# Attention followed by two mixtures of experts on one core: values in three buffers, keys and queries loaded three units ahead, weight loads shifted by unit

## The chip, the cores and the metric

The kernel runs on one core of one Trainium2 chip. The metric is the device time of one execution in microseconds (us). Three executions of the kernel before took 487.59, 489.71 and 493.68 us, a median of 489.71 us.

## The reference

The inputs are q, k and v of shape (4, 8, 576, 64) in float32, so 4 batches and 8 heads of 576 positions.

1. **Attention.** Each head has two softmax attentions that are added. One works on queries, keys and values averaged over groups of 4 positions (144 of them), its output repeated four times. The other is local: a query sees the keys less than 4 positions away. The result is read as x, 2304 tokens by 512.
2. **Soft mixture (called MoE1 here).** logits = x @ phi with 32 slots; a softmax over tokens forms 4 slot inputs for each of 8 experts; each expert computes relu(s @ w1) @ w2 with w1 512x1024 and w2 1024x512; a softmax over slots mixes the slot outputs back into tokens.
3. **Top-2 mixture (MoE2).** A noisy router picks two of 8 experts for each token; each expert computes relu(x @ w1) @ w2 for its tokens, weighted and added into the output, 2304 by 512.

All 16 weight matrices of MoE1 (2 MB each in float32) are read, and 16 more for MoE2.

## The kernel before

**Units and periods.** Attention works on 16 units, each one batch and a pair of heads. Loop variable `p` (L592) runs from -1 to 14; a turn of it is called a period here. Each period goes through the order written out by hand in `SEQ` (L19). Every name there is a step with an offset (table `BL`, L554): step `f` with offset `o` works in period `p` on unit `p - o`. So one period holds parts of four units. After the loop, `TSEQ` (L21) is the hand-written order of the tail, which finishes units 13 to 15 and goes over into MoE1.

**Steps that matter here.**
- `ld` (`load`, L186): four DMAs that bring keys and queries of a unit, two heads each, in rows of 256 bytes, into tile `ld`, which has two buffers. Offset -2: in period p it loads unit p+2. It is the second name of `SEQ`. `load(0)` is issued ahead of the loop.
- `A0`, `A1` (`a_pe`, L230; offset -1): TensorE transposes the keys (A0) and the queries (A1) of unit p+1 out of `ld`.
- `lV` (`load_v`, L202; offset -1): four DMAs (five or six for a few units) bring the values of unit p+1 into one of two buffers `Vs`, unit u into `Vs[u % 2]`. It stands near the end of `SEQ`, behind `DP`.
- `VD` (`v_pe`, L266; offset 1) and `DP` (`d_pe`, L407; offset 1) are the steps that read the values: the averaged values, and the local attention's product.
- `W` (`flush`, L580): issues as many entries of the list `todo` as `NW[p]` says, here 1 in every period from p = 0. An entry is half of a matrix of MoE1, 1 MB. Eight matrices (16 halves) are on the list (`NPRE = 8`); 15 are issued in the loop and the last by the `W` of `TSEQ`.
- `SU_`, `ST`, `SS`, `SK`, `SE`: work on one whole batch for the slot softmax, so in one period of four each, from p = 5.

**Small loads.** Eight small DMAs (two router weights, six pieces of the noise) are issued one for each period from p = 5 (L595), at the start of the period. `phi` is loaded at the start of p = 0.

**Queues.** All these loads are issued by SyncE's queue (SP) in program order. A DMA whose buffer is not free yet makes SP wait, and everything behind it in the order too.

**After attention.** Step `R2` of `TSEQ` gives the memory of attention's buffers to `ring2` (L629): three more matrices of MoE1 (tiles w8a to w10b) are loaded there, each as soon as the tiles that lay there have been read. The last five matrices go through `ringa` and `ringb` (tile `wr`), buffers that come free as MoE1 uses the first matrices. `hidden` (L793) and `second` (L818) are the two layers of MoE1 on TensorE, expert after expert. Behind MoE1 come the router and MoE2 (`tile2`, L1047).

Of the kernel before, what the change touches and what calls it, by code (L numbers as in the profile page):

```python
# [7 lines left out]
F32 = mybir.dt.float32  # L8
# [7 lines left out]

CAP = 640

SEQ = """DM ld S DD A0 M a00 a01 A1 a110 XA a100 SD EL a101 ST a111 SK CP SS EX W VD EP01 MD V0 EP00 EP10 SU_ LG CD EP11  # L19
EP V1 LA ED0 DX SU KD ED1 DP lV x1 x0 DQ1 X0 SE DQ0 RD P0 X1 P1""".split()  # L20
TSEQ = """S:15 DD:13 XA:13 DM:14 CP:14 W EP01:14 EP00:14 SD:15 M:15 EL:15 EP10:14 EX:15 EP11:14 CD:14 ED0:14 MD:15 SU:15 VD:14 DP:14 V0:14 V1:14 EP:13  # L21
ED1:14 P0:15 P1:15 DD:14 DX:15 LG:13 X0:13 RD:15 x0:14 DM:15 x1:14 CP:15 LA:13 EP00:15 X1:13 EP01:15 EP11:15
CD:15 EP10:15 XA:14 ED0:15 VD:15 DP:15 V0:15 V1:15 ED1:15 DD:15 EP:14 x0:15 x1:15 LG:14 X0:14 XA:15 LG:15 EP:15 X0:15 LA:14
# [2 lines left out]
ON_V = ['k1', 'd1', 'a101', 'a111', 'v0']  # L26
ON_V_END = ['P0', 'k1', 'v0', 'v1']

NW = [1] * 15

SPIN = [2, 0, 1, 14, 6, 1]
NPRE = 8
# [6 lines left out]
def attn_moe_moe_kernel(ctx: ExitStack, tc: tile.TileContext, q, k, v, moe_phi, moe_w1, moe_w2,  # L39
                        w_gate, w_noise, noise, w1, w2, out, dbg=None):  # L40
    nc = tc.nc
    B, H, S, D = q.shape
    NT = B * S
    DM = H * D
# [11 lines left out]
    NU = len(units)  # L56
# [61 lines left out]
    with ExitStack() as tctx:  # L118
# [6 lines left out]
        a1 = actx.enter_context(tc.tile_pool(name="a1", bufs=1))  # L125
        wka = actx.enter_context(tc.tile_pool(name="wka", bufs=2))
        a2 = actx.enter_context(tc.tile_pool(name="a2", bufs=1))
        wk = actx.enter_context(tc.tile_pool(name="wk", bufs=2))
# [24 lines left out]
        P = a2.tile([128, NG, 64], F32, name="P")  # L153
        PdT = a2.tile([128, 2, 2, 144], F32, name="PdT")
        Vd = a2.tile([128, 2, 128], F32, name="Vd")
        Vs = [(a1, a2)[i].tile([128, 5, 2, D], F32, name=f"V{i}") for i in range(2)]
        four = a2.tile([128, 9, 32], F32, name="four")
        for a in range(2):
            as_ = slice(64 * a, 64 * a + 64)
# [24 lines left out]
        LD, KD, DQ, SD, SS, SB, PD, PL, XL, XT, XK = ({} for _ in range(11))  # L184

        def load(u):  # L186
            b, hp = units[u]
            t = ldp.tile([96, 2, 6, 2, D], F32, name="ld")
            for i, src in enumerate((k, q)):
                for h in range(2):  # L190
                    nc.sync.dma_start(out=t[:, i, :, h], in_=src[b, 2 * hp + h].rearrange("(c p) d -> p c d", c=6))
            LD[u] = t
# [8 lines left out]

        def load_v(u):  # L202
            b, hp = units[u]
            V = Vs[u % 2]
            hv = v[b, 2 * hp:2 * hp + 2]
            for h in range(2):
                for g2 in range(2):

                    j0, j1 = int(u == h == g2 == 0), 5 - int(u == NU - 1 and h == g2 == 1)
                    rows = slice(64 * g2, 64 * g2 + 64)  # L210
                    t0 = 58 * (2 * j0 + g2) - 3
                    nc.sync.dma_start(out=V[rows, j0:j1, h], in_=bass.AP(
                        tensor=hv.tensor, offset=hv.offset + (h * S + t0) * D,
                        ap=[[D, 64], [116 * D, j1 - j0], [1, D]]))
                    if j0:
                        nc.sync.dma_start(out=V[3:64, 0, h], in_=hv[h, 0:61])
                    if j1 < 5:
                        nc.sync.dma_start(out=V[64:121, 4, h], in_=hv[h, S - 57:S])

# [45 lines left out]

        def v_pe(u):  # L266

            V = Vs[u % 2]
            XL[u] = [ps.tile([128, 512], F32, name=n) for n in ("xa", "xb")]
            t = XL[u][0][:, 290:418]  # L270
            for d in range(2):
                for c in range(4):
                    nc.tensor.matmul(t[32 * c:32 * c + 32], four[:, 5 * d + c],
                                     V[:, c + d].rearrange("p h d -> p (h d)"), start=(d == 0), stop=(d == 1),
                                     skip_group_check=True)
            nc.tensor.matmul(XL[u][1][0:32, 290:418], four[:, 4], V[:, 4].rearrange("p h d -> p (h d)"), start=True,
                             stop=True, skip_group_check=True)
# [128 lines left out]

        def d_pe(u):  # L407
            b, hp = units[u]
            V = Vs[u % 2]
            xl = XL[u]  # L410
            PTv = PT.rearrange("p j g (a i h) -> p j g h a i", a=2, h=2)
            for j in range(5):
                for g in range(2):
                    gs = slice(64 * g, 64 * g + 64)
                    for h in range(2):
                        nc.tensor.matmul(xl[g][64 * h:64 * h + 64, 58 * j:58 * j + 58], V[gs, j, h],
                                         PTv[gs, j, g, h, :, 0:HQ], start=True, stop=True, skip_group_check=True)
# [131 lines left out]
        def ok(u):  # L549
            return 0 <= u < NU  # L550

        load(0)

        BL = {"ld": (load, -2, ()), "lV": (load_v, -1, ()), "EP": (e_pe, 2, ()), "LG": (logit_pe, 2, ()),  # L554
              "X0": (e_evac, 2, (0,)), "X1": (e_evac, 2, (1,)), "LA": (logit_add, 2, ()),
              "S": (b_s, 0, ()), "SD": (b_d, 0, ()), "M": (soft_m, 0, ()), "EL": (soft_s, 0, ()), "EX": (soft_e, 0, ()),
              "SU": (soft_l2, 0, ()), "P0": (soft_p, 0, (0,)), "P1": (soft_p, 0, (1,)), "MD": (soft_d1, 0, ()),
# [8 lines left out]
        for j in range(2):  # L566
            BL[f"a0{j}"] = (a_evac, -1, (0, 0, j))
            for h in range(2):
                BL[f"a1{h}{j}"] = (a_evac, -1, (1, h, j))
        for i in range(2):  # L570
            BL[f"x{i}"] = (d_evac, 1, (i,))
        MW, todo = {}, []
# [7 lines left out]
        def flush(n=99):  # L580
            for _ in range(min(n, len(todo))):
                todo.pop(0)()

        for i in range(NPRE):
            mload(ORDW[i], ringa if i < 3 else ringb)
        small = [(wgn[:, :, E * i:E * i + E], w.rearrange("(k p) e -> p k e", p=128))
                 for i, w in enumerate((w_gate, w_noise))]
# [4 lines left out]
        for p in range(-1, NU - 1):  # L592
            if p == 0:
                nc.sync.dma_start(out=phi, in_=moe_phi.rearrange("(k p) s -> p k s", p=128))
            if p >= 5 and small:  # L595
                o, i = small.pop(0)
                nc.sync.dma_start(out=o, in_=i)
            if p == 1:
                nc.gpsimd.memset(zero, 0.0)
            b4, r4 = divmod(p - 5, 4)  # L600
            for nm in SEQ:
                f, off, a = BL.get(nm, (None, 99, ()))
                if off is None:
                    if 0 <= b4 < B and r4 == a:
                        f(b4)
                elif ok(p - off):
                    f(p - off, *a)
                if nm == "W" and p >= 0:
                    flush(NW[p])
                if p == -1 and nm == "lV":  # L610
                    nc.gpsimd.memset(PT, 0.0)
                    nc.gpsimd.memset(Vd[:, 1], 0.0)
                    nc.gpsimd.memset(PdT[:, 1], 0.0)
                if p == -1 and nm == "DQ1":
                    nc.vector.memset(P, 0.0)
            if p == 0:
                hot(NHOT[0])
                nc.vector.tensor_scalar(trib, jp, 0.0, None, op0=ALU.is_gt)
                consts()
# [58 lines left out]
        for nm in TSEQ:  # L678
# [4 lines left out]
            else:  # L683
                n, u = nm.split(":")
                f, off, a = BL[n]
                f(int(u), *(a if off is not None else ()))
# [569 lines left out]
    for e in range(E):  # L1256
# [36 lines left out]
        elif nx is not None:  # L1293
# [4 lines left out]
            for n in range(NTILE):  # L1298
                i = s0 + n // 9
# [25 lines left out]
        for sl, n0, n1 in SCAT:  # L1325
            if sl // 5 == e:
                f = fill[sl % 5]
# [82 lines left out]
```

## Time and profile before

| | |
|---|---|
| median of three executions | 489.71 us |
| profiled execution: time, span | 488.25 us, 486.5 us |
| TensorE matmul, busy in the span | 458.1 us (94%) |
| VectorE, ScalarE, GpSimd, busy | 275.1, 270.5, 221.9 us |
| bytes moved by SP's queue | 90.50 MB |
| mean granted TensorE clock | 0.993 |

Busy times include pipelining and are no proof that an engine is the limit: the share is an average over stages with different limits. The stages by the trace: attention up to 159.94 us (first matmul of MoE1), MoE1 up to 192.42 us, router and first dispatch up to 207.94 us, then MoE2. In the rows further down, SPq is SyncE's queue issuing a DMA, PE is TensorE's matmuls and PEld its weight loads; a bracket at the end of a row gives how long the engine had been idle before and what released it.

### The profile page before, as it was taken

What the parts mean: (1) busy time and instruction counts of PE and PEld (TensorE: products, weight loads), DVE (VectorE), ACT (ScalarE), POOL (GpSimd) and SP (SyncE); (2) the same over time, 40 slices, a digit from 0 to 9 for tenths busy, and PEclk for the clock granted to TensorE, in tenths of its full rate; (3) what the DMA queues carried; (4) which work ended last, traced back from release to release, by engine and by line L of the source; (5) the groups of instructions that cost most, each with busy time, mean ns of one, the idle gap of its engine ahead of it and who ended that gap; (6) DMA issues with size and microseconds to landing.
All of it is one profiled execution on the core that took longest, in us unless ns stands there. A gap on an engine that the chain in (4) does not pass through costs nothing.

```text
span 486.5 us, 12430 instructions
## 1 busy us (share of the span) xinstructions
PE 458.1 (94%) x4765; PEld 355.7 (73%) x4765; DVE 275.1 (57%) x703; ACT 270.5 (56%) x699; POOL 221.9 (46%) x321
## 2 busy tenths in 40 slices
PE   6999998899888999999999999999999999999992
PEld 5788877778765543577777887887887877878882
DVE  6888676887875321886487463382552634615300
ACT  2687777777765112674484453672755646727310
POOL 7897667577631201084766677222222222212232
PEclk9999899999999999999999999999999999999998
DMA  8999999899979999999986843799958855333333
GB/s 161 234 245 204 249 207 204 222 224 232 251 212 377 378 394 395 372 341 353 355 236 183 244 67 62 214 357 265 274 98 220 201 129 139 45 43 45 44 44 46
DMA packets 107977, 104.19 MB, mean 214 GB/s; under 512 B 67722, under 2 KB 77642, under 8 KB 107914
## 3 DMA queue, kind: packets, MB, share of 16 engines
q1 hardware_dynamic: 101002, 90.50, 62.5%
q0 software_dynamic: 6912, 12.85, 17.6%
q8 instruction: 40, 0.66, 0.6%
q14 instruction: 23, 0.19, 0.1%
HBM read 83.60 MB, written 19.73 MB: 212 GB/s over the span
## 4 chain that ended last, share of the span: by engine, by line
PE 42%; issue 8%; POOL 2%; POOLq 2%; DVE 1%; DMA 1%; ACT 1%; DVEq 0%
PE y L1061 34%; PE gx L878 2%; PE h L1041 2%; POOL out_dram L1080 2%; POOLq L1086 1%; PE gx L1041 1%; DMA out_dram<-ys,idx 1%; PE xs L944 1%; DVE hl L1043 1%; PE xs L1022 0%; PE xs L941 0%; ACT ys L1072 0%; DVE wlo L1033 0%; PE gx L958 0%; ACT hh L1042 0%
## 5 line engine op out<-in xcount | busy, mean ns | idle before, releaser
L1061 PE MATMUL y<-whi,hl 128*128 128x512 f32 x320 | 127.3, 398 | 0.0
L1061 PE MATMUL y<-whi,hh 128*128 128x512 f32 x320 | 126.6, 396 | 0.4 <-ACT hh L1042 0.4
L1061 PE MATMUL y<-wlo,hh 128*128 128x512 f32 x320 | 126.6, 396 | 0.0
L1080 POOL DMA_INDIRECT out_dram<-ys,idx x40 | 64.6, 1614 | 108.5 <-ACT ys L1072 62.6
L1072 ACT ACTIVATE ys<-y,gt 128x512 f32<-128x512 f32 x40 | 27.4, 686 | 83.7 <-issue 46.9
L1033 DVE TENSOR_TENSOR wlo<-wr,whi 128x512 fp32r<-128x512 f32 x64 | 42.0, 692 | 49.3 <-ACT whi L1030 41.7
L1061 PEld LDWEIGHTS y<-wlo,hh 128*128 128x128 f32 x320 | 60.1, 188 | 12.9 <-issue 1.0
L1061 PEld LDWEIGHTS y<-whi,hl 128*128 128x128 f32 x320 | 60.1, 188 | 12.3 <-issue 2.1
L1061 PEld LDWEIGHTS y<-whi,hh 128*128 128x128 f32 x320 | 60.2, 188 | 11.8 <-ACT hh L1042 0.6
L1007 POOL DMA_INDIRECT tab<-stk,pos x36 | 35.8, 994 | 11.5 <-issue 10.4
L1043 DVE SCALAR_TENSOR_TENSOR hl<-h,hh 128x256 fp32r<-128x256 f32 (+1 forms) x64 | 31.4, 490 | 16.0 <-ACT hh L1042 10.6
L1043 DVE SCALAR_TENSOR_TENSOR hl<-gx,hh 128x256 fp32r<-128x256 f32 (+1 forms) x64 | 31.2, 488 | 10.7 <-ACT hh L1042 7.4
L1030 ACT ACTIVATE whi<-wr 128x512 fp32r<-128x512 f32 x64 | 36.9, 625 | 0.2
L1042 ACT ACTIVATE hh<-gx 128x256 fp32r<-128x256 f32 (+1 forms) x64 | 28.1, 439 | 15.0 <-PE gx L1041 12.0
L1042 ACT ACTIVATE hh<-h 128x256 fp32r<-128x256 f32 (+1 forms) x64 | 28.0, 437 | 12.5 <-PE h L1041 9.5
L236 PE MATMUL t<-idf,ld 96*128 96x96 f32 x192 | 23.7, 270 | 11.8 <-DMA ld<-in_q_dram 5.6
L1079 POOL MEMSET spacer<- 1x1 f32 x40 | 13.5, 338 | 40.9 <-issue 40.9
L236 PEld LDWEIGHTS t<-idf,ld 96*128 96x128 f32 x192 | 18.8, 153 | 16.4 <-DVE fa L166 4.3
L254 POOL TENSOR_TENSOR s<-Q 64x288 f32<-64x288 f32 x31 | 29.3, 945 | 2.4
L336 POOL TENSOR_TENSOR P<-El,su 64x350 f32<-64x350 f32 x31 | 24.4, 787 | 11.4 <-DVE Vd L226 4.9
L224 ACT ACTIVATE PT<-t 64x384 f32<-64x384 f32 (+1 forms) x64 | 25.9, 429 | 6.2 <-PE t L378 5.0
L926 DVE TENSOR_TENSOR oh<-iot,R 128x256 fp32r<-128x256 f32 (+2 forms) x50 | 20.5, 446 | 12.7 <-PE xs L944 10.3
(312 smaller groups left out, 877.9 us busy)
## 6 DMA issues: line engine op xcount, KB each, us to landing
wr<-in_moe_w_dram SPq DMA_DIRECT2D x88, 256.0 KB
wr<-in_moe_w_dram SPq DMA_DIRECT2D x40, 512.0 KB
wr<-in_moe_w_dram SPq DMA_DIRECT2D x16, 1024.0 KB
out_dram<-zero SPq DMA_DIRECT2D x20, 256.0 KB
V<-in_v_dram SPq DMA_DIRECT2D x62, 80.0 KB
ld<-in_k_dram SPq DMA_DIRECT2D x32, 144.0 KB
ld<-in_q_dram SPq DMA_DIRECT2D x32, 144.0 KB
XT<-tab SPq DMA_DIRECT2D x5, 320.0 KB
```

Of the source, the lines that this page charges most:

```text
L224: nc.scalar.activation(dst, src, AF.Copy)
L236: nc.tensor.transpose(t[:, 96 * c:96 * c + 96], ld[:, i, 3 * j + c].rearrange("p h d -> p (h d)"), idf[0:96, 0:96])
L254: nc.gpsimd.tensor_tensor(q2, q4[:, :, 0:2], q4[:, :, 2:4], op=ALU.add)
L336: eng.tensor_tensor(P[as_, :, HQ * a:HQ * a + KW], El[as_], su[as_, :, None].to_broadcast([64, NG, KW]), op=ALU.mult)
L1007: st = nc.gpsimd.indirect_dma_start(out=tab, out_offset=bass.IndirectOffsetOnAxis(ap=pos[:, c, i:i + 1], axis=0), in_=stk[:, i].bitcast(F3 ...
L1030: nc.scalar.activation(whi[:, kk], wb(kk), AF.Copy)
L1033: eng.tensor_tensor(wlo[:, kk], wb(kk), whi[:, kk].bitcast(F32), op=ALU.subtract)
L1042: nc.scalar.activation(hh[:, f], h, AF.Relu)
L1043: nc.vector.scalar_tensor_tensor(hl[:, f], h, 0.0, hh[:, f].bitcast(F32), op0=ALU.max, op1=ALU.subtract)
L1061: nc.tensor.matmul(y, l[:, kk, ts_], r_[:, kk], start=(m == 0), stop=(m == 23))
L1072: nc.scalar.activation(ys, YS.pop((e, ti)), AF.Copy, scale=gt[:, ti:ti + 1])
L1080: st = nc.gpsimd.indirect_dma_start(out=out, out_offset=bass.IndirectOffsetOnAxis(ap=idx[:, ti:ti + 1], axis=0), in_=ys, in_offset=None, c ...
```

## The change

Five edits. `ld` loads unit p+3 in place of p+2, `load(1)` joins `load(0)` ahead of the loop, and the step stands behind `A1`; `lV` and `W` move up to stand right behind it. The values get three buffers, one in each of three pools (`wk`, `a1`, `a2`). `NW` becomes 0 for p = 0, 1 for p = 1 to 12 and 2 for p = 13 and 14, 16 in all, which leaves none for the `W` of the tail. The eight small loads are issued four each at the start of p = 13 and p = 14. Tile `ld` keeps two buffers.

```diff
-SEQ = """DM ld S DD A0 M a00 a01 A1 a110 XA a100 SD EL a101 ST a111 SK CP SS EX W VD EP01 MD V0 EP00 EP10 SU_ LG CD EP11
-EP V1 LA ED0 DX SU KD ED1 DP lV x1 x0 DQ1 X0 SE DQ0 RD P0 X1 P1""".split()
+SEQ = """DM S DD A0 M a00 a01 A1 ld lV W a110 XA a100 SD EL a101 ST a111 SK CP SS EX VD EP01 MD V0 EP00 EP10 SU_ LG CD
+EP11 EP V1 LA ED0 DX SU KD ED1 DP x1 x0 DQ1 X0 SE DQ0 RD P0 X1 P1""".split()
...
-NW = [1] * 15
+NW = [0] + [1] * 12 + [2] * 2
...
-        Vs = [(a1, a2)[i].tile([128, 5, 2, D], F32, name=f"V{i}") for i in range(2)]
+        Vs = [(wk, a1, a2)[i].tile([128, 5, 2, D], F32, name=f"V{i}", bufs=1) for i in range(3)]
...
-            V = Vs[u % 2]
+            V = Vs[u % 3]
...
         load(0)
-
-        BL = {"ld": (load, -2, ()), "lV": (load_v, -1, ()), "EP": (e_pe, 2, ()), "LG": (logit_pe, 2, ()),
+        load(1)
+
+        BL = {"ld": (load, -3, ()), "lV": (load_v, -1, ()), "EP": (e_pe, 2, ()), "LG": (logit_pe, 2, ()),
...
-            if p >= 5 and small:
+            for _ in range(4 if p >= NU - 3 else 0):
                 o, i = small.pop(0)
                 nc.sync.dma_start(out=o, in_=i)
```

The line with `u % 3` stands in `load_v`, `v_pe` and `d_pe`.

## Rows read from the trace of the kernel before

**Rows 1.** The chain that ended last, in order of time: its first piece.

```profile
207.94 0.53 issue
```

**Rows 2.** Stretches: length, busy PE, PEld, DVE, ACT, POOL (instructions), clock, DMA share, GB/s.

```profile
280.00:486.00 206.00, 197.86 (x1028) 159.09 (x1026) 85.57 (x186) 104.85 (x224) 64.32 (x77) 0.99 0.59 135
24.39:39.16 14.77, 14.77 (x319) 13.32 (x317) 12.36 (x33) 12.53 (x40) 13.58 (x21) 1.00 1.01 231
93.54:103.78 10.24, 9.11 (x176) 7.21 (x177) 8.25 (x19) 6.96 (x22) 5.74 (x10) 1.00 1.03 219
112.69:129.37 16.68, 15.15 (x318) 13.39 (x316) 14.12 (x35) 13.22 (x44) 11.58 (x17) 1.00 1.17 234
```

**Rows 3.** TensorE's waits from 40 to 132 us: total, times, longest.

```profile
PE t L236 <- DMA ld<-in_q_dram: 5.3, 7, 1.1
PE t L236 <- DMA ld<-in_k_dram: 1.0, 2, 0.6
```

**Rows 4.** Timeline of TensorE: start, length, line, operation, idle before and releaser.

```profile
5.86 1.19 PE L236 MATMUL t<-idf,ld 96*128 96x96 f32 x6 [0.29 <-DMA ld<-in_q_dram]
...
48.08 0.69 PE L236 MATMUL t<-idf,ld 96*128 96x96 f32 x6 [0.33 <-DMA ld<-in_k_dram]
49.47 0.85 PE L236 MATMUL t<-idf,ld 96*128 96x96 f32 x4 [0.71 <-DMA ld<-in_q_dram]
...
130.90 0.80 PE L236 MATMUL t<-idf,ld 96*128 96x96 f32 x6 [0.81 <-DMA ld<-in_q_dram]
```

**Rows 5.** Stretches: the period with the low clock, and the end of the loop.

```profile
48.08:58.34 10.26, 9.43 (x159) 8.32 (x159) 6.56 (x18) 6.99 (x24) 6.27 (x9) 0.83 0.92 220
137.50:145.00 7.50, 6.14 (x136) 5.35 (x129) 5.02 (x14) 4.15 (x13) 2.26 (x3) 1.00 0.60 158
```

**Rows 6.** DMA issues on the page: tile, queue, count, size of each.

```profile
wr<-in_moe_w_dram SPq DMA_DIRECT2D x16, 1024.0 KB
...
V<-in_v_dram SPq DMA_DIRECT2D x62, 80.0 KB
ld<-in_k_dram SPq DMA_DIRECT2D x32, 144.0 KB
```

**Rows 7.** Stretches: only 256-byte rows on the queue; only weights on it.

```profile
4.00:10.00 6.00, 5.14 (x55) 4.27 (x55) 4.41 (x12) 0.82 (x2) 3.60 (x7) 1.00 1.04 175
160.00:190.00 30.00, 30.00 (x507) 13.76 (x506) 7.40 (x24) 5.72 (x11) 3.81 (x10) 1.00 1.03 386
```

**Rows 8.** Timeline of SP's queue: when DMAs were issued.

```profile
68.94 0.60 SPq L597 DMA_DIRECT2D nz<-in_moe_noise_dram  x1
...
125.14 1.35 SPq L191 DMA_DIRECT2D ld<-in_q_dram  x2
...
130.61 0.60 SPq L102 DMA_DIRECT2D wr<-in_moe_w_dram  x1
137.59 2.61 SPq L212 DMA_DIRECT2D V<-in_v_dram  x4
...
141.20 3.41 SPq L104 DMA_DIRECT2D w8a<-in_moe_w_dram  x4
...
161.07 35.81 SPq L104 DMA_DIRECT2D wr<-in_moe_w_dram  x44
```

**Rows 9.** SP's waits from 4 to 137.7 us: total, times, longest.

```profile
SPq L212 <- PE xb L416: 9.4, 6, 6.4
```

**Rows 10.** Timeline of TensorE: first use of the values; start and end of MoE1.

```profile
19.41 0.65 PE L273 MATMUL xa<-V,four 128*32 128x128 f32 x16
...
159.94 2.80 PE L800 MATMUL hp<-wr,sinT 128*32 128x256 f32 x48
...
186.19 6.30 PE L824 MATMUL yacc<-wr,hz 128*32 128x512 f32 x21
192.42 0.77 PE L758 MATMUL ct<-idf,LK 128*128 128x128 f32 x5
```

**Rows 11.** Weight loads of TensorE in MoE1: waits from 160 to 193 us.

```profile
PEld yacc L824 <- DMA wr<-in_moe_w_dram: 3.4, 6, 0.7
```

More of the change, by code (lines that the diff above doesn't have):

```diff
@@ L266, in v_pe @@
         def v_pe(u):
-            V = Vs[u % 2]
+            V = Vs[u % 3]
             XL[u] = [ps.tile([128, 512], F32, name=n) for n in ("xa", "xb")]
@@ L408, in d_pe @@
             b, hp = units[u]
-            V = Vs[u % 2]
+            V = Vs[u % 3]
             xl = XL[u]
```

## The prediction

> **What bounds the kernel now.** I read the chain of waits first. It can be followed back only to 207.94 us [rows 1]; from 280 us on TensorE is busy for 197.86 of 206 us [rows 2]. So MoE2 is work of TensorE that the change does not touch, and the change moves the end by as much as it moves the end of MoE1.
>
> I then cut attention into periods at the transpose of the keys (A0), and read the busy times of each stretch. From 24.39 to 39.16 us two periods ran with TensorE busy all the time: 14.77 us, 7.39 each [rows 2]. That is what a period costs when no load is late. Later ones are longer: the ten from 39.16 to 129.37 us (both are bounds of stretches in [rows 2], and starts of an A0) took 90.21 us, 9.0 each. Two of the ten carry the batch's slot product, with 9.11 us of busy TensorE in place of 7.39 [rows 2]. So TensorE alone would need 8 x 7.39 + 2 x 9.11 = 77.3 us, and 12.9 us are excess.
>
> The waits say what part of the excess is the loads': 5.3 us for queries and 1.0 for keys, nine waits, 6.3 us together [rows 3]. The granted clock shows a second part. In the period from 48.08 us it was 0.83 [rows 5]: a third of 10.26 us, 3.5 us, at 1.2 GHz, right after two waits for keys and queries [rows 4]. That costs at most half of 3.5, 1.7 us. The other 4.9 us have no single owner.
>
> The DMA side. A period moves 4 x 144 + 4 x 80 KB in rows of 256 bytes (0.92 MB) and one half matrix (1.05 MB) [rows 6]. Loads of 256-byte rows nearly alone ran at 175 GB/s, weights alone at 386 [rows 7]. So a period asks for 0.92/175 + 1.05/386 = 5.2 + 2.7 = 7.9 us of a full DMA, against 7.39 of TensorE, and 7.39 to 9.11 with the slot work. From 112.69 to 129.37 us the DMA share was 1.17 and a period took 8.3 us [rows 2]: there the loads set the pace. The two limits lie within a few tenths of each other.
>
> The Trainium skill (DMA: Bandwidth & Descriptors, section Why small descriptors are slow) counts 11 cycles in place of 8 for a 256-byte descriptor. By that, an estimate from 386 GB/s, these rows would run at 281 GB/s and a period would ask for only 6.0 us. The row disagrees, with 175 GB/s [rows 7], and the measurement decides; my sum goes by it.
>
> **The change, part by part.**
>
> *Loads of keys and queries, one unit further ahead.* The same four DMAs, issued behind A1, which frees the buffer. The tile still has two buffers, so SP now waits for A1 in each period, with lV and W behind it. None of these is urgent: ld is needed almost two periods later (2 x 7.39 less the 1.4 us from A0 to A1 [rows 4], 13.4 us), lV a period and a half later, W in MoE1. What stands in the queue ahead of a unit's keys and queries shrinks. For unit 15, whose queries were issued at 125.14 and awaited until 130.90 us [rows 8, 4], two half matrices (2 x 2.7 = 5.4 us), one unit's values (0.33/175 = 1.9 us) and the eight small loads go behind it. A small load holds the queue for 0.60 us [rows 8], at most 4.8 us for eight; the trace has no row for the engines' time, so the lower bound is near nothing. The keys and queries of unit 15 thus arrive 7.3 to 12.1 us sooner, and TensorE may come up to that much sooner without waiting. For early units it is two half matrices and a unit's values, 7.3 us; the DMA then loses about 0.2 us a period to TensorE (7.9 against a mean of 7.7), 2 us over ten. So I take all nine waits away: **-6.3 us**. Bounds: 0 if the loads stay the pace, -12.9 if the whole excess goes.
>
> *Low clock.* The fall followed waits that go. It can happen elsewhere, so I take **-1.0** of 1.7 us.
>
> *Three buffers for the values, lV earlier.* Before, lV waited for DP of the unit two back: 9.4 us in six waits, one of them 6.4 us, from the half matrix at 130.61 to V at 137.59 us [rows 8, 9]. In that gap the DMA ran dry: share 0.60 in 7.5 us [rows 5], 3.0 us of DMA idle. With a third buffer V is free when lV comes. On TensorE this is worth nothing by itself. For unit 0, V is now queued behind load(2), which waits for A1 of unit 0 until 7.1 us [rows 4]; with four issues of load(2) between, V is issued near 9 us and first used at 19.41 us [rows 10]: **0**. The cover is that distance of 10 us.
>
> *Half matrices and small loads moved to the last two periods.* No keys or queries load there: 0.59/175 = 3.4 us for each of two periods come free, against one more half matrix (2.7 us) and four small loads. The half matrix of the tail, which stood behind the late V, goes into the gap. They are needed in MoE1 and the router, which begin 29 us after the loop's last half matrix [rows 8, 10]: **0**. Were the gap not there, one more half matrix ahead of w8a would cost 2.7 us.
>
> *New wait of SP on A1.* When SP runs ahead, the DMA can run dry. Between 0 (about a period's worth of DMAs is queued) and +3.0 us (what the one long wait of SP for a buffer left idle [rows 5]). The nearest row is that of the start, where SP would wait first: the DMA is full there [rows 7], so I take **0**.
>
> *MoE1.* It ran from 159.94 to 192.42 us [rows 10], and its last matmuls waited 3.4 us for weights [rows 11]. The last five matrices (10.5 MB, 27.2 us at 386 GB/s) are loaded into buffers that its first matmuls free, so they start 1.1 us behind it, at 161.07 us [rows 8]. If attention ends 7.3 us sooner, this load starts 7.3 us sooner, provided that w8a to w10b (6.3 MB, 16.3 us) are done by then: they started at 141.20 us [rows 8], and now follow at once on the earlier loads, into the 3.0 us of idle DMA and whatever is saved before. Thus MoE1 keeps its 32.5 us, the router and the zero fills behind it move along, and the gain reaches the end.
>
> **Sum:** 488.25 - 6.3 - 1.0 = 480.95, **481.0 us**. This starts from the profiled execution's own 488.25 us, which lies 1.5 us below the median of 489.71; against the median it is -1.8%.
>
> **Rivals.**
>
> *The waits move into MoE1 (chance 0.22).* The bytes are the same and the DMA share was near 1 in most of attention. Then only idle DMA counts: attention ends sooner, but weights come late by what was gained. The gain is the hole of 3.0 us: 485.3 us. For it: the weights were the last wait in MoE1 already [rows 11]. Against: shares of 0.92 and below [rows 5] show idle DMA in the middle too.
>
> *TensorE alone sets the pace (0.18).* If the lateness came from late issue and not from want of bandwidth, all 12.9 us go: 475.3 us. For it: two periods at 7.39 us with a full DMA [rows 2]. Against: 8.3 us a period at share 1.17. The figure of the Trainium skill for 256-byte rows would lead here too; [rows 7] speak against it.
>
> *Slower: the clock falls in MoE1 (0.10).* Attention ends 7 us sooner but the weights do not, so TensorE waits 7 + 3.4 us between pairs of matmuls, as it did for 186.19 us on [rows 10]. In the period from 48.08 us waits of 0.33 and 0.71 us were followed by 3.5 us at 1.2 GHz. Each such fall costs up to 1.7 us; two or three up to the router's end make +4: 492 us. If the 22 us from 186 to 208 us all ran at 1.2 GHz, the price is up to 11 us, 499 us. It decides once the waits break up TensorE's work more than those of 0.7 us in MoE1 do now, for which the clock stayed at 1.00. The Trainium skill (TensorE: Matmul & The Clock Gate, section HAM oscillation) describes this case, waits for DMA that bring the array back to 1.2 GHz; [rows 4, 5] agree, [rows 10, 7] show waits without a fall.
>
> **How the numbers follow.** The forecast has 0.50, with its own range of 478 to 484 us. The prediction is 481 us. The range of 474.5 to 488.5 us takes in the first two rivals and leaves out the slower one and a part of the edge below. A measurement of this kernel can tell about 2% from no change: below 479.9 or above 499.5 us. Below lie a good third of the forecast (0.18) and nearly all of the second rival (0.17): 0.35 faster. Above lies the upper part of the last rival: 0.05 slower. Same: 0.60.
>
> **What would show it.** In the changed profile: no waits of L236 for `ld` after 40 us, or under 1.5 us in total; regular periods of 7.4 to 7.8 us; V issued without waiting for L416; a DMA share near 1 from 130 to 145 us; MoE1 beginning at about 152.6 us and lasting 32 to 33. If L236 still waits, the load term is wrong; if MoE1 is longer by what attention won, the first rival holds; if the clock is under 1.00 between MoE1 and MoE2, the last one does.

## The result and the profile after

The changed kernel took 494.08 us (median of 20 executions, 490.28 to 498.25), the kernel before 490.77 us beside it (20 executions, 487.19 to 494.87): a ratio of 1.0073, 95% interval 1.0048 to 1.0099. It is 0.7% slower, where 481.0 us was forecast and 488.5 was the upper end of the range. The profiled execution took 492.57 us with a span of 490.8 and a mean granted clock of 0.974 (before 0.993).

Same five stretches of both kernels (stretch; length; busy time of PE, PEld, DVE, ACT, POOL with instructions; clock; DMA share; GB/s). First the kernel before:

```profile
4.00:24.00 20.00, 18.58 (x259) 15.24 (x261) 15.21 (x43) 9.93 (x32) 16.03 (x26) 1.00 1.02 211
24.00:48.00 24.00, 23.05 (x482) 20.39 (x478) 19.95 (x50) 18.89 (x60) 20.98 (x30) 1.00 0.99 228
48.00:120.00 72.00, 65.64 (x1288) 56.22 (x1290) 55.04 (x142) 53.29 (x173) 48.54 (x71) 0.98 1.00 222
120.00:156.00 36.00, 31.49 (x595) 24.84 (x595) 26.30 (x74) 25.14 (x81) 15.07 (x21) 1.00 0.95 272
156.00:192.00 36.00, 36.00 (x551) 16.43 (x548) 9.47 (x33) 5.93 (x12) 5.55 (x29) 1.00 1.03 388
```

Then the changed kernel:

```profile
4.00:24.00 20.00, 17.42 (x194) 14.04 (x197) 16.02 (x39) 8.33 (x25) 14.24 (x23) 1.00 0.93 168
24.00:48.00 24.00, 23.66 (x534) 21.30 (x525) 19.86 (x52) 20.29 (x68) 21.61 (x32) 1.00 0.92 234
48.00:120.00 72.00, 66.29 (x1186) 57.50 (x1187) 50.62 (x132) 49.48 (x159) 45.66 (x66) 0.89 0.93 215
120.00:156.00 36.00, 34.80 (x704) 28.76 (x703) 28.90 (x76) 27.82 (x90) 19.14 (x27) 0.99 0.86 250
156.00:192.00 36.00, 35.20 (x547) 16.49 (x545) 10.98 (x41) 7.37 (x19) 4.09 (x27) 1.00 1.04 394
```

From 24 to 156 us TensorE is busier than before (a part of it at the low clock), but up to 156 us the DMA share fell from 0.95-1.02 to 0.86-0.93 in the same stretches. Length times GB/s, summed over the five rows, is 49.4 MB before and 47.6 MB after.

TensorE's waits from 24 to 140 us (total, times, longest) answer to [rows 3]. The waits for `ld` are gone; what is left is "issue", idle time for which the profile shows no releaser:

```profile
PE S L292 <- issue: 4.5, 3, 2.1
PE xb L416 <- issue: 1.5, 1, 1.5
```

SP's longest entry in the same stretch, which answers to [rows 9]: the loads of keys and queries now wait for A1. In the kernel before, none of their waits there is on TensorE.

```profile
SPq L191 <- PE t L236: 13.6, 9, 3.2
```

TensorE's timeline (start, length, line, operation, idle before): the first and the last A0 of ten periods, a stall of "issue" and the A0 behind it, the start and end of MoE1, which answer to [rows 10]:

```profile
41.14 1.21 PE L236 MATMUL t<-idf,ld 96*128 96x96 f32 x12
...
77.26 0.86 PE L292 MATMUL S<-K,Q 128*64 128x35 f32 x13 [2.15 <-issue]
79.06 2.18 PE L236 MATMUL t<-idf,ld 96*128 96x96 f32 x12
...
133.68 1.21 PE L236 MATMUL t<-idf,ld 96*128 96x96 f32 x12
...
161.60 2.80 PE L801 MATMUL hp<-wr,sinT 128*32 128x256 f32 x48
...
190.46 6.14 PE L825 MATMUL yacc<-wr,hz 128*32 128x512 f32 x21
196.53 0.77 PE L759 MATMUL ct<-idf,LK 128*128 128x128 f32 x5
```

Ten periods took 92.5 us, no less than before. MoE1 started at 161.60 (before 159.94) and ended at 196.53 (192.42): 1.66 us lost in attention and 2.45 in MoE1, 4.1 together. From there to the end of the span is 294.3 us, before 294.1. So in this profile the whole loss is made by the end of MoE1. The waits of MoE1 for weights grew too, against [rows 11]:

```profile
PEld yacc L825 <- DMA wr<-in_moe_w_dram: 5.8, 9, 1.2
```

### The profile page after: what moved, and what is told of

It reads as the page before. It is cut to its first block, busy times and chain, and to the rows that moved or that the text cites. A ratio compares the mean times of both kernels' runs of the same rounds, so it can differ in the third digit from the quotient of the medians.

```text
span 490.8 us, 12417 instructions
## 1 busy us (share of the span) xinstructions
PE 465.7 (95%) x4765; PEld 362.8 (74%) x4765; DVE 275.9 (56%) x703; ACT 270.9 (55%) x699; POOL 221.3 (45%) x321
## 4 chain that ended last, share of the span: by engine, by line
PE 41%; issue 8%; POOL 2%; POOLq 2%; DVE 1%; ACT 1%; DMA 1%; DVEq 0%
PE y L1062 34%; PE gx L879 2%; PE h L1042 2%; POOL out_dram L1081 2%; POOLq L1087 1%; PE gx L1042 1%; DMA out_dram<-ys,idx 1%; PE xs L945 1%; DVE hl L1044 1%; PE xs L1023 0%; PE xs L942 0%; ACT ys L1073 0%; DVE wlo L1034 0%; ACT hh L1043 0%; PE gx L959 0%
## 5 line engine op out<-in xcount | busy, mean ns | idle before, releaser
L292 PE MATMUL S<-K,Q 128*64 128x35 f32 x640 | 24.1, 235 | 5.8 <-issue 4.5
L236 PE MATMUL t<-idf,ld 96*128 96x96 f32 x192 | 24.2, 287 | 4.9 <-DMA ld<-in_k_dram 4.5
L292 PEld LDWEIGHTS S<-K,Q 128*64 128x64 f32 x640 | 24.0, 151 | 6.6 <-issue 6.4
```

What stands on the lines that cost most here:

```text
L292: nc.tensor.matmul(s[64 * a:64 * a + 64, KW * g:KW * g + KW], Q[:, c0:c0 + 32].rearrange("p i h -> p (i h)"), K[:, c0:c0 + KW], start=Fals ...
```

## The experiments

Eighteen runs were made. In the quoted expectations B says that the bytes SP's queue has moved set the end of MoE1, D that SP's new wait for A1 makes them late, C that TensorE's stalls and the clock set the time, and H that small loads ahead of the last values spoil the handover to MoE1; S and W are as each text puts them. First what all profiles show together, since many verdicts rest on it. "MB" is the sum over 4 to 192 us as above; "order" is the order in which SP goes round the three loads of a period, wherever that round begins.

| kernel | order | ratio (95%) | MoE1 from | to | MB |
|---|---|---|---|---|---|
| before | ld W V | 1 | 159.94 | 192.42 | 49.4 |
| changed | ld V W | 1.0073 (1.0048-1.0099) | 161.60 | 196.53 | 47.6 |
| again | ld V W | 1.0049 (1.0013-1.0085) | 158.81 | 194.83 | 48.4 |
| hold_w | ld V | 1.0368 (1.0296-1.0439) | 148.69 | 213.38 | 41.1 |
| ld3 | ld V W | 1.0044 (1.0010-1.0078) | 163.40 | 200.72 | 46.2 |
| w_ahead | ld V W | 1.0149 (1.0103-1.0195) | 166.80 | 199.33 | 46.8 |
| ld_only | ld W V | 1.0028 (0.9995-1.0061) | 163.68 | 197.31 | 47.5 |
| v_only | ld V W | 1.0119 (1.0064-1.0174) | 165.13 | 197.74 | 47.3 |
| w_only | ld W V | 1.0062 (1.0018-1.0106) | 160.78 | 194.36 | 48.9 |
| ld_v | ld V W | 0.9999 (0.9958-1.0041) | 158.48 | 190.90 | 50.1 |
| nw_only | ld W V | 1.0019 (0.9988-1.0050) | 164.72 | 196.84 | 47.7 |
| small_only | ld W V | 0.9951 (0.9914-0.9989) | 161.88 | 194.68 | 48.5 |
| w0back | ld V W | 1.0092 (1.0052-1.0131) | 155.40 | 194.18 | 48.7 |
| s_behind | ld V W | 1.0105 (1.0045-1.0166) | 158.60 | 198.59 | 47.0 |
| w0_s_behind | ld V W | 1.0102 (1.0037-1.0167) | 162.76 | 201.60 | 45.9 |
| w_early | ld V W | 1.0029 (0.9992-1.0065) | 163.18 | 199.47 | 46.6 |
| w_front | ld W V | 0.9930 (0.9892-0.9967) | 161.01 | 193.53 | 49.0 |
| front_s | ld W V | 0.9894 (0.9840-0.9947) | 157.86 | 190.09 | 50.3 |
| front_b | ld W V | 1.0009 (0.9965-1.0054) | 170.92 | 203.44 | 45.2 |
| swap | ld W V | 0.9945 (0.9915-0.9974) | 152.63 | 187.83 | 51.2 |

The last two columns lie on one line: a least-squares fit of the 20 profiles gives 2.54 us for each MB missing, and none is off it by more than 0.6 us. That is 394 GB/s, the rate of weights alone (386 in [rows 7], 394 in the changed kernel from 156 us). The line does not say which of the two leads. In nw_only and front_b MoE1 took 32.1 and 32.5 us, no more than before, so there it ended late because attention did, and the bytes are missing because MoE1's buffers came free late. In the changed kernel and in swap MoE1 took 34.9 and 35.2 us and waited for weights. Single profiles scatter more than medians (front_b's execution took 501.05 us, its median is 495.47; ld3's 497.99 and 493.18), so the verdicts go by the ratios.

**The changed kernel again, unaltered (again).**

> The changed kernel once more, unaltered, to see which of its traits come back. Theory D (SP's new wait for A1 runs the DMA dry, so the weights of MoE1 come late): SP waits for A1 again 12 to 18 us in all, the DMA share from 24 to 132 us is again about 0.90 against 0.97 before, MoE1 ends at 195 to 198 us; time 493 to 495 us. Theory C (TensorE's stalls without a releaser, and the low clock after them, set the time): stalls marked issue of 4 to 8 us in attention and 14 to 20 us of low clock come back at the same places; 493 to 495 us too. If the stalls are elsewhere or gone and the time is the same, C falls.

Measured: 1.0049 (1.0013 to 1.0085). The loss is real; two measurements of one kernel differ by 0.0024, so smaller differences are not read below. But this second profile (491.08 us) loses its time in another place than the first. SP's wait for A1, then the clock and the DMA share in attention:

```profile
SPq L191 <- PE t L236: 3.3, 3, 2.2
24.00:140.00 116.00, 111.03 (x2271) 95.84 (x2269) 95.61 (x248) 92.82 (x303) 85.58 (x122) 1.00 0.96 223
48.00:120.00 72.00, 68.44 (x1372) 59.39 (x1371) 58.88 (x153) 57.12 (x183) 53.49 (x78) 1.00 0.96 218
```

SP waited for A1 for 3.3 us in place of 13.6, where D expected 12 to 18: the long wait is a trait of the first profile and not of the kernel, so D as it was put falls. Stalls of "issue" add up to 4.3 us, most of it at other times than in the first profile, so C as it was put falls too. TensorE's timeline, first and last A0 of ten periods and the first use of the last unit's values, then the clock behind it:

```profile
40.56 1.21 PE L236 MATMUL t<-idf,ld 96*128 96x96 f32 x12
...
122.98 0.55 PE L236 MATMUL t<-idf,ld 96*128 96x96 f32 x4
...
143.82 1.08 PE L273 MATMUL xa<-V,four 128*32 128x128 f32 x16 [2.95 <-DMA V<-in_v_dram]
```

```profile
144.00:150.00 6.00, 5.34 (x79) 3.99 (x78) 1.23 (x3) 1.32 (x3) 0.00 (x0) 0.50 0.98 392
```

Ten periods took 82.4 us here, 7.8 less than before, which is about the gain that was forecast. It was lost again behind them: TensorE waited 2.95 us for the values of unit 15, ran at 1.2 GHz for some 10 us after that (0.86 granted from 120 to 156 us), and MoE1 took 36.0 us.

**No weights in the loop (hold_w).** All 16 half matrices go to the `W` of the tail.

```diff
-NW = [0] + [1] * 12 + [2] * 2
+NW = [0] * 15
```

> The changed kernel without any half matrix in attention; all 16 are issued in the tail, so MoE1 must wait some 40 us longer and the whole takes 520 to 535 us. Only attention up to the tail is read. C with a full DMA as the cause: with no weights queued the stalls marked issue fall under 1 us in all and the clock stays at 1.00 from 24 to 130 us, periods of 7.4 us (8.9 with the slot product), the transposes of unit 15 near 117 us. C without it (the stalls lie in TensorE's own program): the same 4 to 6 us at the same places. D says nothing on the stalls, but SP's waits for A1 grow to 30 us or more, since TensorE alone is the limit then.

Measured: 1.0368, 508.63 us, less than the 520 to 535 expected. This run separates attention's pace from the end. Stretch from 48 to 120 us, then TensorE's first and last A0 of ten periods, and MoE1:

```profile
48.00:120.00 72.00, 72.00 (x1498) 62.72 (x1495) 62.98 (x165) 60.99 (x200) 57.44 (x83) 1.00 0.57 114
```

```profile
41.65 1.21 PE L236 MATMUL t<-idf,ld 96*128 96x96 f32 x12
...
119.50 1.21 PE L236 MATMUL t<-idf,ld 96*128 96x96 f32 x12
...
148.69 2.80 PE L801 MATMUL hp<-wr,sinT 128*32 128x256 f32 x48
...
213.38 0.77 PE L759 MATMUL ct<-idf,LK 128*128 128x128 f32 x5
```

Ten periods took 77.85 us (77.3 was worked out for TensorE alone), with no stall of "issue" and no fall of the clock from 24 to 140 us. Attention ended 11.25 us sooner than before, and the kernel is 18 us longer, since MoE1 waits for weights. So an earlier end of attention is not by itself an earlier end of the kernel. Nor do the stalls order the times of the other kernels: from 24 to 140 us nw_only has none and its profiled execution took 493.54 us, ld_v has 6.6 us of them and took 486.97.

**A third buffer for keys and queries (ld3).** Room is made by laying `fi` and `fa` into `P` and `mtmp` into `K`, and a narrower scratch tile.

```diff
-        ldp = actx.enter_context(tc.tile_pool(name="ldp", bufs=2))
+        ldp = actx.enter_context(tc.tile_pool(name="ldp", bufs=3))
```

> The changed kernel with three buffers for the keys and queries in place of two, so that SP waits for nothing; room is made by three scratch tiles that share other tiles' memory. D: SP's 15 us of waits for A1 go, the DMA share from 24 to 132 us is 0.96 or more, MoE1 ends 4 to 9 us sooner than in the changed kernel (187 to 192 us), time 485 to 490 us. C: more DMAs are queued, the stalls marked issue stay at 4 us or more or grow, time 493 us or more.

Measured: 1.0044, no gain, a miss for D. SP's wait for A1 is gone but for 1.5 us from 24 to 140 us, and the kernel is as slow as the changed one. So this wait is not what makes it slow.

**Half matrices ahead of A1 (w_ahead).**

```diff
-... a01 A1 ld lV W a110
+... a01 W A1 ld lV a110
```

> The changed kernel with W moved from behind lV to ahead of A1, so that the half matrix of a period is queued ahead of the load that waits for A1, not behind it. D: SP still waits for A1, but the DMA has 2.7 us more to do meanwhile, so its share from 24 to 132 us rises to 0.94 or more and the time falls to 489 to 492 us. C: no change, 493 to 495 us.

Measured: 1.0149, slower, a miss for D. For SP the round is still ld, V, W, since A1 issues nothing on SP; its wait for A1 is 1.6 us. In the last two periods two half matrices each now stand ahead of the values, and TensorE waited 5.57 us for those of unit 15.

**The loads alone (ld_only), the values alone (v_only), half matrices and small loads alone (w_only)**, each made on the kernel before.

```diff
 ld_only
+        load(1)
-        BL = {"ld": (load, -2, ()), ...
+        BL = {"ld": (load, -3, ()), ...
-DM ld S ... A1 a110
+DM S ... A1 ld a110
 v_only (three buffers)
-A1 a110 ... DP lV x1
+A1 lV a110 ... DP x1
 w_only
+NW = [0] + [1] * 12 + [2] * 2
+            for _ in range(4 if p >= NU - 3 else 0):
```

> The kernel before with the first part of the change alone: ld loads unit p+3, stands behind A1, and load(1) stands ahead of the loop; values, half matrices and small loads as before. Theory B (the end of MoE1 is set by the bytes that SP's queue has moved; attention's speed does not count): bytes from 4 to 192 us within 0.6 MB of the 49.5 MB of before, so the end of MoE1 within 1.5 us of 192.4 and the time within 1.5 us of before, although TensorE's waits for ld go. Theory C (TensorE's stalls and its clock set the time): the waits for ld go, the stalls marked issue stay under 3 us as before, and the time falls by 4 to 7 us.

> The kernel before with the second part alone: three buffers for the values, lV behind A1. B: SP no longer waits for DP, no hole in the DMA from 137 to 145 us, so up to 1 MB more is moved by 192 us and the time falls by 0 to 3 us. C: TensorE still waits for ld, as much or more, since V is now queued closer behind ld; no change or up to 2 us slower.

> The kernel before with the last part alone: no half matrix in p = 0, two in each of p = 13 and 14, the eight small loads there too. B: the first half matrix (1.05 MB) is missing from the first 24 us and cannot be made up, 1.05/0.39 = 2.7 us, so the end of MoE1 comes 2 to 3.5 us later and the time is 2 to 3.5 us longer. C: fewer DMAs are queued in the middle, so stalls and waits shrink: the same time or up to 3 us shorter.

Measured: 1.0028, 1.0119 and 1.0062. Not one part gains alone. w_only loses about what B expected. The loads, to which 6.3 us of the forecast belong, give nothing by themselves. The values moved up are the worst part: this edit alone turns the round from ld, W, V into ld, V, W. It was costed at nothing, and v_only had been expected to do better than it did.

**Loads and values together, the rest as before (ld_v).**

```diff
-NW = [0] + [1] * 12 + [2] * 2
+NW = [1] * 15
-            for _ in range(4 if p >= NU - 3 else 0):
+            if p >= 5 and small:
```

> The changed kernel with half matrices and small loads as before (one half matrix in each unit from p = 0, one small load in each from p = 5). B: the first half matrix is back in the first 24 us and the last values stand behind one half matrix only, so 1 MB more than in the changed kernel is moved by 192 us, MoE1 ends 2 to 3.5 us sooner than there, time 489.5 to 492 us. C: more DMAs queued than in the changed kernel, stalls and falls of the clock as many or more: 493 to 496 us.

Measured: 0.9999 (0.9958 to 1.0041), 489.85 us, as B has it. These are the edits that carry the whole forecast gain of 7.3 us, with half matrices and small loads as before, and they give nothing; the interval leaves them 2 us at most. Against the changed kernel's two measurements ld_v is 0.5 to 0.7% better, so in this order of the loads the later weights and small loads do cost.

**The half matrices and the small loads apart (nw_only, small_only), on the kernel before.**

```diff
 nw_only
+NW = [0] + [1] * 12 + [2] * 2
 small_only
+            for _ in range(4 if p >= NU - 3 else 0):
```

> The kernel before with the half matrices moved alone: none in p = 0, two in each of p = 13 and 14, small loads as before. Theory B (the end of MoE1 follows the bytes that SP's queue has moved): the bytes from 4 to 48 us fall by 0.8 to 1.2 MB against before and part of it is missing at 192 us; the time is 1.5 to 3.5 us longer than before. Rival S (the small loads in the last two units are what costs, by holding up the last values): no change, within 1 us of before.

> The kernel before with the small loads moved alone: four each at the start of p = 13 and 14, half matrices as before. B: the bytes by 192 us stay within 0.4 MB of before, the time within 1.5 us. S: the last values come late, TensorE waits 2 to 6 us for V at its step VD of unit 15 and the clock falls after it, 2 to 4 us longer than before.

Measured: 1.0019 and 0.9951. Neither loses on the kernel before by itself, and the small loads at the end even gain a little, against what was expected; both together (w_only, 1.0062) do lose.

**The changed kernel with its first half matrix back (w0back), with the small loads behind the values (s_behind), with both (w0_s_behind).**

```diff
 w0back, w0_s_behind
+NW = [1] * 14 + [2]
 s_behind, w0_s_behind: moved from the start of p = 13 and 14 to their end
             for _ in range(4 if p >= NU - 3 else 0):
                 o, i = small.pop(0)
```

> The changed kernel with the first half matrix put back: one in each unit from p = 0 to 13, two in p = 14; small loads late, as in the changed kernel. B: 0.7 to 1 MB more from 4 to 48 us than in the changed kernel, MoE1 ends 2 to 3 us sooner than there (192 to 194 us), time 490 to 492 us. S: the last values are as late as in the changed kernel, 493 to 495 us.

> The changed kernel with the eight small loads still in p = 13 and 14, but at the end of each of these periods, behind the values and the half matrices, not ahead of them. Theory H (handover: what stands ahead of the last values in SP's queue delays them, with them the end of attention and the loads of w8a to w10b): the last values are issued 4 to 8 us sooner than in the changed kernel (138.84 us there), w8a before 141 us, time 1.5 to 4 us below the changed kernel, ratio to before 0.996 to 1.004. Theory W (the half matrix taken from the start is what costs, handover does not): as the changed kernel, ratio 1.004 to 1.009.

> As the run before, and the first half matrix put back (one in each unit from p = 0 to 13, two in p = 14). H: ratio to before 0.993 to 1.001, 3 us or more below the kernel with the half matrix back and the small loads ahead (1.0092). W: 1.000 to 1.003, the same as that kernel ought to have had. If it stays at 1.006 or more, both fall.

Measured: 1.0092, 1.0105 and 1.0102. None of them mends it, so H falls, and the missing first half matrix is not the cause by itself.

**Values ahead of keys and queries, two half matrices in the first unit (w_front, made from ld_v; front_s with the small loads behind in the last two; front_b, the shifted half matrices alone on the kernel before).**

```diff
 w_front, front_s
-... A1 ld lV W a110
+... A1 lV ld W a110
 w_front, front_s, front_b
+NW = [2] + [1] * 14
```

> The changed kernel with small loads as before, two half matrices in p = 0 and one in each later unit (none left for the tail), and lV ahead of ld, so that the values of unit 0 are not behind the wait for A1. B: the opposite of the change's shift; the bytes from 4 to 48 us are 0.5 to 1 MB above those of the kernel with ld and values changed alone, by 192 us 50.2 MB or more, MoE1 ends at 189 to 191 us, time 486 to 489.5 us, although TensorE waits for ld more. C (TensorE's stalls and clock set the time): keys and queries come later by 2.7 us in every unit, waits for ld of 5 us or more in attention, 492 us or more.

> The kernel with two half matrices in p = 0 and values ahead of keys and queries (ratio 0.993), with the small loads moved to the end of p = 13 and 14. H and W: the small loads leave the middle units and stand behind the last values, so no worse, 0 to 2 us better: ratio 0.988 to 0.994. If small loads in the last units cost wherever they stand: 0.996 or more.

> The kernel before with two half matrices in p = 0, one in each later unit and none in the tail; nothing else changed. H: the last values wait for DP as before and stay late, so the handover is as before; the half matrix that left the tail takes nothing off the way of the last values: ratio 0.997 to 1.003. W: a half matrix more at the start is won as it was lost in the changed kernel: ratio 0.992 to 0.996.

Measured: 0.9930, 0.9894 and 1.0009. The first two are faster than both kernels; front_s, 486.41 us beside 493.09, has the lowest ratio of the study. front_b shows that the two early half matrices give nothing on the kernel before. front_s and w0_s_behind differ by the exchange of `ld` and `lV` and the half matrices, and by 2% in time. The last two runs take these apart.

**The exchange alone (swap), the half matrices alone (w_early), each on the changed kernel.**

```diff
 swap
-... A1 ld lV W a110
+... A1 lV ld W a110
 w_early
-NW = [0] + [1] * 12 + [2] * 2
+NW = [2] + [1] * 14
```

> The changed kernel with one exchange in the order: `A1 lV ld W` in place of `A1 ld lV W`. Nothing else is changed: no half matrix in the first unit, two in each of the last two, the small loads at the start of the last two. Theory S (the loss is made at the start: load(2) stands ahead of the first values and waits for A1, so the queue runs dry between 4 and 24 us): the values, which have a free buffer, go out while load(2) waits. GB/s from 4 to 24 us rise from 167 to about 190 at least (233 needs the two half matrices as well), which is 0.4 MB or 1.0 us by the line of 2.52 us per MB, and later units too have their values queued ahead of SP's wait for A1: ratio to before 0.997 to 1.003, so under that of the changed kernel. Theory W (the half matrices put off are the loss, since a full queue of work that is not urgent is what keeps the DMA busy while SP waits): no half matrix comes earlier here, ratio as the changed kernel's, 1.005 to 1.010, and 4 to 24 us stay at 165 to 180 GB/s.

> The changed kernel with NW = [2] + [1] * 14 in place of [0] + [1] * 12 + [2] * 2: two half matrices in the first unit, one in each later one, and nothing else changed (order `A1 ld lV W`, small loads at the start of the last two). Theory W: the two matrices (2.1 MB) stand in the queue from the first unit on and cover SP's waits for A1; 4 to 24 us rise to about 220 GB/s or more, MoE1 ends at 191 to 194 us and the ratio to before is 0.990 to 0.998, near that of the kernel with the exchange in the order too. Theory S: the two come behind load(2)'s wait for A1, so the first 24 us gain less than the 2.1 MB (190 to 210 GB/s), each later unit's values still stand behind the wait; ratio 1.000 to 1.007.

Measured: swap 0.9945 (0.9915 to 0.9974), w_early 1.0029 (0.9992 to 1.0065). The exchange of two names turns the loss into a gain; against the changed kernel's two measurements, 1.0073 and 1.0049, that is 1.0 to 1.3%. The ratio is even a little under what S expected, but S had the place wrong. w_early lies in S's range: the early half matrices alone change little. The five stretches of swap:

```profile
4.00:24.00 20.00, 16.79 (x189) 13.63 (x192) 16.38 (x39) 8.22 (x25) 14.03 (x22) 1.00 0.97 170
24.00:48.00 24.00, 23.75 (x537) 21.39 (x532) 19.93 (x52) 20.26 (x69) 21.58 (x32) 1.00 1.03 234
48.00:120.00 72.00, 69.03 (x1358) 60.06 (x1362) 57.77 (x149) 55.68 (x180) 52.34 (x77) 0.98 1.11 243
120.00:156.00 36.00, 34.58 (x659) 25.73 (x655) 25.77 (x79) 23.24 (x77) 14.41 (x38) 1.00 0.89 293
156.00:192.00 36.00, 35.24 (x570) 15.04 (x566) 8.28 (x29) 7.22 (x17) 3.50 (x8) 1.00 1.04 393
```

Up to 24 us it moved 170 GB/s, like the changed kernel's 168, not the 190 expected. The 3.6 MB that swap has more come from 48 to 156 us, at 243 for 215 and 293 for 250 GB/s. SP's timeline (start, length, line, DMA) shows the pace of the queue. These rows are the loads of the values of unit 4 and of unit 12, eight rounds of the three loads apart: the kernel before, the changed kernel, its second profile, swap.

```profile
37.74 2.70 SPq L212 DMA_DIRECT2D V<-in_v_dram  x4
...
110.83 2.65 SPq L212 DMA_DIRECT2D V<-in_v_dram  x4
```

```profile
37.16 4.64 SPq L212 DMA_DIRECT2D V<-in_v_dram  x4
...
110.24 4.74 SPq L212 DMA_DIRECT2D V<-in_v_dram  x4
```

```profile
36.97 4.92 SPq L212 DMA_DIRECT2D V<-in_v_dram  x4
...
110.71 4.54 SPq L212 DMA_DIRECT2D V<-in_v_dram  x4
```

```profile
32.35 4.15 SPq L212 DMA_DIRECT2D V<-in_v_dram  x4
...
99.61 2.65 SPq L212 DMA_DIRECT2D V<-in_v_dram  x4
```

A round took 9.14 us before, 9.13 and 9.22 in the two profiles of the changed kernel, and 8.41 in swap. All nine profiles with keys and queries three units ahead, three buffers for the values and the order ld, V, W lie at 8.99 to 9.83 us, the three with V, ld, W (swap, w_front, front_s) at 8.41 to 8.71. SP's waits do not make this difference. Between the rows of its timeline from 24 to 120 us SP stood idle for 13.3 us in the first profile of the changed kernel, 5.8 in the second, 2.7 in w_early and 4.7 in swap: in the second profile and in w_early it issued nearly without a break and kept the slow pace all the same. What differs is how long the four loads of the values hold SP, 4.1 and 4.8 us a unit in the changed kernel's profiles (units 4 to 11) and 3.1 in swap, and how full the DMA is meanwhile: its share from 48 to 120 us is 0.93 and 0.96 against 1.11. Two rows point at a reason. The first is of hold_w, 2 us in which the values are the last loads in the queue. The second is of the second profile, the end of one unit's values, which SP issued from 45.95 to 51.34 us, with the half matrix behind them:

```profile
47.00:49.00 2.00, 2.00 (x63) 1.76 (x54) 1.42 (x6) 1.62 (x7) 1.86 (x4) 1.00 0.66 149
```

```profile
50.00:52.00 2.00, 2.00 (x44) 1.74 (x43) 1.93 (x6) 1.93 (x6) 1.80 (x3) 1.00 0.57 104
```

In both the DMA's share is about 0.6. So the values may fill it badly by themselves, and may do better with other loads right behind them; no run tests this.

MoE1 of swap, and its wait for weights:

```profile
152.63 2.80 PE L801 MATMUL hp<-wr,sinT 128*32 128x256 f32 x48
...
187.83 0.77 PE L759 MATMUL ct<-idf,LK 128*128 128x128 f32 x5
```

```profile
PEld yacc L825 <- DMA wr<-in_moe_w_dram: 6.0, 9, 1.2
```

Attention ends at the time that the forecast gave for it, 152.6 us. MoE1 lasts 35.2 us in place of 32.5, so of 7.3 us 4.6 reach its end, and 1.7 more are lost behind it (295.8 us to the end of the span, before 294.1). The profiled execution took 485.42 us.

Over all runs the order divides them: the ten runs that go round ld, V, W with weights in the loop have ratios from 0.9999 to 1.0149, 1.0076 in the mean; the eight variants that go round ld, W, V lie from 0.9894 to 1.0062, 0.9980 in the mean. Other edits differ within the two groups, so this is support, and the pair of swap and the changed kernel is the proof that the order counts.

## Why the prediction was wrong

**The -6.3 us for the loads, on a DMA that needs 7.9 us a period: the step that failed.** The waits of L236 for `ld` went, all nine [rows 3]. But that was worth 6.3 us only if the DMA kept up with TensorE to within 0.2 us a period. Its 7.9 us were added up from two rates, each measured with one kind of load nearly alone [rows 7], and left the order out. In the changed kernel a round of the three loads took 9.13 us, in its second profile 9.22, as long as before (9.14). So the queue came to its end no sooner: the last values were issued at 138.84 and 137.52 us, before at 137.59 [rows 8]. The loads stayed the pace, which the prediction had as its bound of 0, and ld_v, with these edits alone, is at 0.9999. Where TensorE did run ahead of the loads, in the second profile with ten periods in 82.4 us, it lost the time again on the last values and on weights; in the first, ten periods took 92.5 us. Exchanging `ld` and `lV` makes a round 8.41 us (swap, ten periods in 83.5, A0 at 41.23 and 124.72 us) and the time 1.0 to 1.3% shorter, 5 to 6 us.

**New wait of SP on A1, taken as 0: not what made the loss.** The first profile of the changed kernel has 13.6 us of it from 24 to 140 us, the second 3.3, ld3 1.5 and w_early 0.3, and w0back has none at 1.0092. The row that the 0 was read from, the start with a full DMA [rows 7], did not answer to it either: there 256-byte rows were queued and no weights.

**MoE1 keeps its 32.5 us: failed.** It took 34.9, in the second profile 36.0. Where attention has not outrun the weights, MoE1 takes 32.1 to 32.8 us (nw_only 32.1, front_s 32.2, ld_v 32.4, small_only 32.8), about its own pace; where it has, MoE1 waits for them (swap 35.2, w0back 38.8, hold_w 64.7). The step's own condition, that the earlier matrices are loaded by then, was not met: w8a was issued at 145.32 us, in the second profile at 143.43, before at 141.20 [rows 8]. This follows from the pace of the queue and from the loads put into the last two periods.

**Half matrices and small loads, taken as 0: too low.** On the kernel before nw_only is at 1.0019 and small_only at 0.9951, but both together (w_only) at 1.0062 (1.0018 to 1.0106), and ld_v, without both, is 0.5 to 0.7% better than the changed kernel's two measurements, 2.5 to 3.6 us. One price is seen in SP's timeline of the changed kernel:

```profile
133.82 4.92 SPq L598 DMA_DIRECT2D nz<-in_moe_noise_dram  x4
138.84 4.83 SPq L212 DMA_DIRECT2D V<-in_v_dram  x4
...
145.32 2.03 SPq L104 DMA_DIRECT2D w8a<-in_moe_w_dram  x4
```

Four small loads held SP for 4.92 us, 1.23 each against the 0.60 of [rows 8], and the last values stand behind them; in the second profile these came 2.95 us late for TensorE. But s_behind, which puts the small loads last, is no better, so their place alone is not what made the loss.

**Low clock, -1.0: wrong.** TensorE was at 1.2 GHz for 17 us between 24 and 140 us, after stalls, where it was 3.4 before. The second profile of the same kernel has none of it there, but some 10 us later on, behind the wait for the last values. How much of the loss the clock makes is not shown.

**The rivals.** Waits that move into MoE1 had part of the mechanism right: MoE1 did get longer. Its price of 485.3 us came from closing one hole in the DMA. That swap's profiled execution took 485.42 us is luck, since there the gain comes from the pace of the whole loop, with another order. In the changed kernel that hole (0.60, [rows 5]) closed only in part:

```profile
137.50:145.00 7.50, 7.50 (x163) 6.12 (x159) 6.75 (x18) 5.07 (x17) 2.69 (x4) 1.00 0.74 206
```

TensorE alone as the pace was seen in hold_w only, without weights. The clock falling in MoE1 did not happen: the clock was 1.00 from 156 to 192 us.

**What stays open.** Why the DMA moves more in one order than in the other. How much of swap's gain comes by way of fewer stalls of TensorE (3.2 us of "issue" against 6.0 and 4.3). Why w0back and s_behind, which each take back a part of the last edits, did not help, while ld_v, which takes back all, did.

## What to carry to other kernels

Where one queue brings everything in order, moving a load forward does not make the queue faster. Ask first what pace the queue keeps as a whole: rates of single kinds of load, measured apart, gave 7.9 us for a round that took 9.1 to 9.2, and the order of the same loads made it 8.4. Take a second profile of the same kernel before a wait is called the cause: 13.6 us of waiting in the first were 3.3 in the second, and the kernel was slow in both. Before a stage is shortened, look at what the next one waits for: here MoE1 is fed by the same queue, and in the changed kernel's two profiles and in swap it took 34.9 to 36.0 us in place of 32.5, waiting for weights. Try the order of the loads before the rest: exchanging two names was worth about as much as the largest of the five edits.

## What the runs showed that was not expected

TensorE stalls of up to 3.1 us for which the profile names no releaser ("issue") come in attention, most of them at L292 and L416, at other times in each kernel. hold_w, with no weights in the loop, has none; nw_only, with weights, has none up to 140 us. A late fetch of TensorE's instructions would fit, but no run tests it. The clock can fall to 1.2 GHz after such a stall. The changed kernel's stretch from 77.50 us, right after the stall of 2.15 us shown above:

```profile
77.50:83.00 5.50, 5.50 (x41) 5.10 (x40) 2.90 (x6) 2.05 (x5) 0.83 (x2) 0.50 0.80 248
```

The Trainium skill (TensorE: Matmul & The Clock Gate, section HAM oscillation) puts such falls down to waits for DMA between matmuls; this row agrees on the fall, but the wait before it has no DMA to its name. The fall at 144 us in the second profile does come behind a wait for a DMA, 2.95 us for the values.
